# A retention and Fourier-mixing kernel: all work behind the first batch goes onto one written list, the third batch multiplies by seven half-size products in two of three groups, and masks are multiplied in place in f16

## The chip, the cores and the metric

The kernel runs on one core of a Trainium2 chip. The metric is the device time of one execution in microseconds (us). The core has five engines: TensorE (PE in the profile) multiplies matrices, VectorE (DVE) and ScalarE (ACT) work on tiles in SBUF and PSUM, GpSimd (POOL) does elementwise work here and issues a few transfers, and SyncE (SP) issues most of the transfers. Each engine runs its own instructions in order and waits for semaphores of the others.

## The reference

Inputs are q, k and v, each [4 batches, 8 heads, 768 positions, 64], and two weights, w_ch1 [512, 2048] and w_ch2 [2048, 512], all f32. The output is [4, 768, 512] in f32.

```python
gamma = 1 - 2 ** (-5 - arange(8)); scale = 1 / 8
for t in range(768):                       # per batch and head
    state = gamma * state + outer(k[t], v[t])
    y[t] = scale * q[t] @ state
x = heads of y side by side                # [4, 768, 512]
mixed = real(fft(fft(x, axis=1), axis=2))
u = x + mixed
un = (u - mean(u)) / sqrt(var(u) + 1e-6)   # over the 512 columns
out = u + relu(un @ w_ch1) @ w_ch2
```

## The kernel before, in words

The rows of a batch are six blocks of 128. A batch passes through these stages; the letters in brackets are those that the list of the change uses for the same work.

Retention, for each of four pairs of heads. `load_unit` (l) loads q, k and v of the pair by three transfers on the queue of SyncE into buffers of the pool `inp`. `cast_unit` (k) casts them to f16 on GpSimd, k with its decay (L441). `t_unit` (t) transposes q and k to `qT` and `kT`; for the first two batches mostly on TensorE with a copy on ScalarE, for the last two by two transposing transfers issued on SyncE's queue (`qTz<-q16z`, L612, and `kT<-kd`, L614). `kv_unit` (s) makes the running state of each block of rows, `wkK` on TensorE and the sum on VectorE (L696). `a_unit` (a) makes the scores in three parts: two matmuls of 256 columns into `wkA` (L667), and VectorE multiplies the 512 columns in PSUM with a f32 mask into the f16 tile `atm` (L670). `y_unit` (y) multiplies the state and the masked scores with q and v (L717, L721), and ScalarE puts the result into `x` (L729).

The Fourier transform. VectorE folds x by its symmetries (fs, fd, fe; L746, L773, L787, L789 with the tile `ee`), `s1_unit` (f) multiplies along the rows (L850), a small matmul makes the zero column (g), ScalarE or VectorE copies the product and its mirrored copy (gr), and `s2_unit` (x) multiplies along the model dimension into `pq` (L1012), with two copies `qn` on ScalarE (L1014), two operations on VectorE that write `u` (L1019 is the first), and two additions of x on GpSimd (L1040, L1042).

The normalisation. `norm_unit` takes statistics on VectorE (n; L1051, L1052) and ScalarE writes the f16 tile `un` (u; L1056). `unT_unit` (U) transposes `un` to `unT`, by TensorE in the earlier batches, by a transposing transfer on SyncE's queue (L1075) later. `rstd_unit` (r) makes the square root and its reciprocal, which are applied at the end.

The two layers. In the first batch `h0_unit` (i; L1109) and then `h_unit` (h; L1092) multiply `unT` with w_ch1: a unit of h makes 128 hidden columns of 384 rows by four matmuls of 384, and the relu goes to ScalarE (L1096) or VectorE (L1098), by the constant `ACT_ROWS`. Batches of this form have two halves of 384 rows. `ch_unit` (c; L1131) multiplies the hidden tile `ht` with w_ch2: four matmuls of 512 columns for each of four parts of a block of rows; VectorE adds u (L1135), and the block is stored through the pool `obp`. The fourth batch has another form: three groups of 256 rows. `hp_unit` (H; L1179) makes two hidden blocks of 256 rows by eight matmuls of 256, with one relu over both (L1184, split in two for the last block of a group). The 256 rows of a group and the 2,048 hidden columns are then treated as a matrix of 2 by 2 blocks, and so is w_ch2, and the product is made from seven half-size products (`p_unit`, p; L1231, eight matmuls of 256 columns each) in place of eight. This needs sums of hidden blocks (`hidden_sums`, L1203), differences of weight blocks (`wsum_unit`, w; L1165, in spare buffers of `inp`), and sums of the products (add, L1235).

What sets the order. The first batch's retention and Fourier work follow a list, `FIRST`, one unit after the other on every engine. Everything behind it is handed to `emit`: each batch's work is a set of streams, each stream has a start and an end as fractions of a batch (the constants `DM0`, `TS0`, `DA1` and their like), the units of all streams are sorted by these times and handed over in that order, and the framework's scheduler may still reorder instructions where nothing depends on them. The casts of all batches and everything of the fourth batch's own two layers, sums and mixing are `held`: each instruction stays behind the instruction of the same engine that stood before it when it was handed over. While the two layers of one batch run, the retention and Fourier work of the next lies between them. The loads of the third and fourth batch wait for the scores of the second pair of the batch before (`a_of`).

Of the kernel before, what the change touches and what calls it, by code (L numbers as in the profile page):

```python
# [11 lines left out]
AF = mybir.ActivationFunctionType  # L12
# [7 lines left out]
P = 128  # L20
# [27 lines left out]
ON_ACT = {'q': (0, 1, 0), 'kv': (1, 1, 1), 'g': (0, 1, 1), 'gr': (0, 0, 0)}  # L48
# [3 lines left out]
TS1 = (-0.040, -0.020, 0.048, 0.585)  # L52
DA0, DA1 = (0.043, 0.161, 0.176, 0.190, 0.284, 0.321), (0.063, 0.067, 0.063, 0.158, 0.168, 0.189)
LD0, LD1 = (0.223, 0.312), (-0.370, 0.140)
HT0 = (0.666, 0.693, 0.632, 0.590)
NPE = 2
WS = (-0.12, -0.02)
# [3 lines left out]
NT = 0.6  # L61
ACT_ROWS = ((2, 5, 6, 7, 8, 9, 10, 14), (0, 3, 6, 7, 9, 10, 11, 12, 14, 15))
# [3 lines left out]
def kernel(  # L66
# [13 lines left out]
    def pool(name, bufs, **kw):  # L80
# [3 lines left out]
    inp = pool("inp", 11)  # L84
# [12 lines left out]
    obp = pool("obp", 3)  # L97
# [52 lines left out]
    def held(unit):  # L150
        def run():
            ins = tc.nc.cur_bb.bb.instructions
            n0 = len(ins)
            unit()
            for n in range(n0, len(ins)):
                m = n - 1
                while m >= 0 and ins[m].engine != ins[n].engine:
                    m -= 1
                if m >= 0:
                    tc.add_manual_dep(ins[n], ins[m].name,  # L160
                                      mybir.DependencyInfo(mybir.DependencyClass.NoSync,
                                                           mybir.DependencyReason.DATA),
                                      reason="casts in turn")
        return run
# [20 lines left out]
    in_of, a_of = {}, {}  # L185
# [420 lines left out]
    def t_unit(b, i):  # L606
        def run():
# [9 lines left out]
            for dst, src in ((qT, q16_of[b, i]), (kT, kd_of[b, i])):  # L617
# [15 lines left out]
                else:  # L633
                    nc.scalar.copy(dst, tq)
        return run

    def a0_unit(b, i, half):
        def run():
            st = at[b, i]
            hp = PAIR_ORDER[i]  # L640
# [848 lines left out]
```

## Time and profile before

| | |
|---|---|
| median of 3 runs | 241.32 us (241.08 to 241.86) |
| the profiled execution | 240.73 us |
| its span, from the first to the last instruction | 238.7 us |
| instructions | 5575 |
| matmuls on TensorE | 2135 |
| operations on VectorE | 460 |
| operations on ScalarE | 273 |
| operations on GpSimd | 148 |

The page of the profile gives the busy time of each engine, the span in forty slices of about 6 us, the chain of work that ended last, and groups of instructions. A group's row has the line of the code, the engine, the operation, the output and input tiles with their shapes, the count, the busy time in us, the mean duration of one in ns, and the idle time of the engine just before, with what ended it. Views of the trace give the same groups by exact shape, what an engine waited for, a list of a chain's parts with their start and length, and the transfers with the time from issue to landing. In the groups of transfers, the three numbers behind the count are the minimum, median and maximum in ns.

### The profile page before, as it was taken

The numbers are of one execution on the slowest core, as the hardware profiler recorded it, in microseconds if no ns is written. First come the engines' busy times: TensorE is split into PE (matmuls) and PEld (weight loads), VectorE is DVE, ScalarE is ACT, GpSimd is POOL, SyncE is SP. The second block draws the span as 40 slices with busy tenths as digits, with TensorE's granted clock in tenths as the row PEclk, the third lists the DMA queues.
The fourth block names the chain that finished last, engine by engine and source line by source line (L and its number), as shares of the span: only waits on it lengthen the run. The fifth ranks groups of instructions, "written<-read, shape, count | busy, mean of one in ns | idle before, by whom it ended". The sixth has DMA issues, their size and how long they took to land.

```text
span 238.7 us, 5575 instructions
## 1 busy us (share of the span) xinstructions
PE 225.4 (94%) x2135; PEld 155.3 (65%) x2135; DVE 187.4 (79%) x460; ACT 125.3 (52%) x273; POOL 81.4 (34%) x148
## 2 busy tenths in 40 slices
PE   0788999999999999999999999999999999999993
PEld 0356779756775646765567446655666468888893
DVE  8789887958898889986886829977895885867473
ACT  5989759674865444840247415822257326072430
POOL 8378802665300097850000826940002410220000
PEclk9999999999999999999999999999999999999999
DMA  7999999999999489979999577696100261031202
GB/s 179 233 270 239 237 206 207 210 251 248 241 235 208 72 191 221 203 138 132 249 279 218 116 161 203 130 138 156 53 3 0 45 154 25 3 110 23 91 0 91
DMA packets 100954, 36.80 MB, mean 154 GB/s; under 512 B 91456, under 2 KB 97984, under 8 KB 100928
## 3 DMA queue, kind: packets, MB, share of 16 engines
q1 hardware_dynamic: 96704, 32.25, 64.2%
q0 software_dynamic: 4224, 4.19, 10.6%
q8 instruction: 17, 0.28, 0.5%
q14 instruction: 9, 0.07, 0.1%
HBM read 27.26 MB, written 6.29 MB: 141 GB/s over the span
## 4 chain that ended last, share of the span: by engine, by line
PE 82%; DVE 6%; DMA 5%; ACT 2%; issue 1%; POOL 1%; SPq 0%; DVEq 0%; ACTq 0%
PE psc L1131 23%; PE psh L1092 21%; PE psh L1179 9%; PE ps L1231 5%; PE psh L1109 3%; PE wkA L667 3%; DMA qTz<-q16z 3%; PE ps L850 3%; DMA k<-in_k_dram 2%; PE wkY L721 2%; PE pq L1012 2%; PE ps L830 1%; DVE atm L539 1%; PE wkY L717 1%; PE wkK L686 1%
## 5 line engine op out<-in xcount | busy, mean ns | idle before, releaser
L1131 PE MATMUL psc<-w,ht 128*128 128x512 f16 x288 | 67.7, 379 | 0.0
L1092 PE MATMUL psh<-unT,w 128*128 128x384 f16 x320 | 59.5, 326 | 0.0
L1040 POOL TENSOR_TENSOR u<-u,x 128x256 f32<-128x256 f32 x21 | 13.3, 635 | 117.1 <-DVE u L1019 104.8
L1131 PEld LDWEIGHTS <-ht 128*128 128x128 f16 x288 | 27.3, 98 | 26.5
L1092 PEld LDWEIGHTS <-w 128*128 128x128 f16 x320 | 29.9, 98 | 15.9 <-DMA unT<-un 0.4
L1096 ACT ACTIVATE ht<-psh 128x384 f16<-128x384 f32 x46 | 22.3, 489 | 23.7 <-PE psh L1092 23.2
L670 DVE TENSOR_TENSOR atm<-wkA,maskp 128x512 f16<-128x512 f32 x36 | 23.6, 680 | 1.7 <-PE wkA L667 1.7
L1184 ACT ACTIVATE ht<-psh 128x512 f16<-128x512 f32 (+1 forms) x24 | 13.7, 571 | 15.6 <-PE psh L1179 11.0
L1179 PE MATMUL psh<-unT,w 128*128 128x256 f16 x192 | 21.6, 273 | 0.0
L1098 DVE TENSOR_SCALAR ht<-psh 128x384 f16<-128x384 f32 x34 | 18.7, 549 | 2.7 <-PE psh L1092 2.5
L1056 ACT ACTIVATE un<-u,stats 128x512 f16<-128x512 f32 x21 | 14.8, 717 | 10.7 <-DVE stats L1052 7.6
L1179 PEld LDWEIGHTS <-w 128*128 128x128 f16 x192 | 18.7, 98 | 2.1
L1135 DVE SCALAR_TENSOR_TENSOR ob<-psc,stats,u 128x512 f32<-128x512 f32 x18 | 13.4, 743 | 8.5 <-PE psc L1131 8.3
L696 DVE SCALAR_TENSOR_TENSOR s<-s,gk,wkK 128x128 f16<-128x128 f16 x48 | 16.1, 336 | 2.4 <-ACT s L692 1.6
L729 ACT ACTIVATE x<-wkY,gexp 128x384 f16<-128x384 f32 x24 | 12.9, 580 | 9.0 <-PE wkY L721 8.9
L1051 DVE BATCH_NORM_STATS2 bst<-u 128x6 f32<-128x512 f32 x21 | 14.4, 686 | 4.0 <-POOL u L1042 3.8
L1231 PEld LDWEIGHTS <-ht 128*128 128x128 f16 x152 | 14.1, 98 | 2.3 <-issue 0.6
L441 POOL TENSOR_SCALAR kd<-k,gexp 128x384 f16<-128x384 f32 x24 | 13.8, 585 | 3.3 <-DMA k<-in_k_dram 3.3
L667 PE MATMUL wkA<-qTz,kT 128*128 128x256 f16 x72 | 13.2, 273 | 0.3 <-DMA qTz<-q16z 0.3
L1042 POOL TENSOR_TENSOR u<-u,x 128x256 f32<-128x256 f32 x21 | 13.3, 635 | 0.0
L1014 ACT COPY qn<-pq 128x128 f32<-128x128 f32 x18 | 4.9, 274 | 15.0 <-PE pq L1012 15.0
L1203 DVE TENSOR_TENSOR ht<-ht 128x512 f16<-128x512 f16 (+2 forms) x21 | 8.1, 385 | 5.9 <-ACT ht L1184 5.6
(194 smaller groups left out, 400.9 us busy)
## 6 DMA issues: line engine op xcount, KB each, us to landing
q<-in_q_dram SPq DMA_DIRECT2D x16, 384.0 KB, 6.0
k<-in_k_dram SPq DMA_DIRECT2D x16, 384.0 KB, 5.6
v<-in_v_dram SPq DMA_DIRECT2D x16, 384.0 KB, 5.7
out_dram<-ob SPq DMA_DIRECT2D x23, 256.0 KB, 2.4
w<-in_moe_w_ch_dram POOLq DMA_DIRECT2D x8, 512.0 KB, 10.9
unT<-un SPq DMA_TRANSPOSE x15, 2.5
kT<-kd SPq DMA_TRANSPOSE x10, 3.0
qTz<-q16z SPq DMA_TRANSPOSE x8, 3.8
```

The costliest lines, as they stand in the source:

```text
L441: kc = nc.gpsimd.tensor_scalar(out=kd[:, :, h2, :], in0=k32[:, h2], scalar1=gkd[:, h0 + h2:h0 + h2 + 1], scalar2=1.0, op0=ALU.mult, op1=AL ...
L667: mm = nc.tensor.matmul(wk[:, c2], st["kT"][:, c, :], st["qT"][:, :, c, :], start=True, stop=True)
L670: nc.vector.tensor_tensor(out=st["atm"][:, 2 * part:2 * part + 2], in0=wk, in1=maskp[:, PAIR_ORDER[i]].unsqueeze(1).to_broadcast([P, 2, 2, ...
L696: nc.vector.scalar_tensor_tensor(out=s16[:, c], in0=s16[:, c - 1], scalar=gk2[:, hp:hp + 1], in1=wk[:, c - c0], op0=ALU.mult, op1=ALU.add)
L1051: nc.vector.bn_stats(bst, u[:, kb, :])
L1056: nc.scalar.activation(un, u[:, kb, :], AF.Identity, bias=stats[:, kb, 0:1], scale=-1.0)
L1092: nc.tensor.matmul(psh, w116[:, cb, fb * P:(fb + 1) * P], unT[:, cb, rt * 384:(rt + 1) * 384], start=(cb == 0), stop=(cb == 3))
L1096: nc.scalar.activation(ht16[:, fb, :], psh, AF.Relu, bias=0.0, scale=-1.0)
L1098: nc.vector.tensor_scalar(out=ht16[:, fb, :], in0=psh, scalar1=-1.0, scalar2=0.0, op0=ALU.mult, op1=ALU.max)
L1131: nc.tensor.matmul(psc, ht16[:, fb, rb3 * P:(rb3 + 1) * P], w216[:, fb, :], start=(fb == 0), stop=(fb == NFB - 1))
L1179: nc.tensor.matmul(psh[:, t], w116[:, cb, fb * P:(fb + 1) * P], unT[:, cb, g * 256:(g + 1) * 256], start=(cb == 0), stop=(cb == 3))
L1231: nc.tensor.matmul(dst, lhsT, rhs[:, c0:c1], start=bool(new and n == 0), stop=(n == 7), skip_group_check=True)
```

## The change

The streams, `emit` and their constants are gone. In their place stands a second list, `LATER`, of 567 small units, in three parts that are divided by a bar. The units of the first part are pinned on every engine in the written order; those of the second part only on GpSimd; those of the third part are `held`, on every engine and on SyncE's queue. The third part begins where the first batch's last output products and the second batch's hidden units meet. A unit's name is its letter, the batch, and further digits for pair, part, group or block; the letter behind @ names the engine that does its copy, relu or mask (a for ScalarE, v for VectorE, b for one half each, s for ScalarE in two halves, d for a transposing transfer). So a300 is the first third of the scores of pair 0 in batch 3, tq30 the transpose of its q, H207 the last hidden unit of group 0 of batch 2, and p201 product 1 of that group. Batches are counted from 0 in these names.

What the units do changes as follows.

- The second and third batch take the form of `hp_unit`: three groups of 256 rows with matmuls of 256 columns, in place of two halves of 384.
- The third batch (batch 2 in the names) uses the seven products in groups 0 and 1, and full products in group 2 (`cg_unit`, C, with `rows_unit`, O). The second batch uses full products in all groups, and the fourth the seven in all groups, as before. The weight differences are made while the second batch runs.
- In the third and fourth batch the masks are done in two steps. ScalarE copies the scores from PSUM to f16 with the scale of each head (two copies of 256 columns for each part), and one operation on VectorE for a pair (`m_unit`, m) multiplies the 1,536 columns in place with one f16 mask, `mask16`. The second batch's pairs keep the f32 mask on VectorE, now a100@v and its like.
- The transposing transfers of q and k are units of their own (`td_unit`; tq and tk), and loads no longer wait for the scores of the batch before.
- `inp` has 7 buffers in place of 11; four tiles' worth of fixed space, `wide`, takes part of the loads of the first batches and then holds the weight differences. `obp` has 2 buffers in place of 3.
- Which engine does a relu or a copy is written at each unit; the sums of hidden blocks (j) and of products (q) are units of their own.

In the counts of instructions: TensorE has 2311 matmuls after, for 2135. Matmuls of 512 columns at L1131 go from 288 to 224, of 384 from 320 to 64, of 256 for hidden units from 192 to 576, and of the seven products' form from 152 to 264 (some of them narrower in the fourth batch's last group, as before). Masks on VectorE from PSUM go from 36 to 12, beside 8 new products of 1,536 columns, and ScalarE gets 48 scaled copies. Relus on ScalarE: 46 to 10 of 384 columns, 27 to 53 of 512, 3 to 29 of 256. Relus on VectorE: 34 to 6 of 384, 6 to 13 of 512, 3 to 7 of 256. SyncE's and GpSimd's instructions keep their number. TensorE's order of matmuls is the same for the first 710.

```diff
+LATER = """
+i00 i01
+|
+i02 i03 U01@v i10 i11 i12 Z i13 U02@a x03 i20 x04 n03 u03 x05 n04 u04 n05 u05 i21 i22 l10 i23
+l11 r00 c0000 l12 k10 c0001 l13 c0002 U03@a c0003 c0010 t10 U04@v c0011 c0012 MK U05@a k11 c0013
+s100 s101 c0020 t11 a100@v c0021 a101@v c0022 a102@v k12 s110 s111 c0023 y100 y101 t12 a110@v
+h010@a a111@v a112@v h011@v k13 s120 s121 h012@v y110 y111 t13 h013@a a120@v a121@v h014@v
+a122@v s130 s131 h015@v PZ y120 y121 h016@a fs10 h017@a fd10 h018@v a130@v h019@a a131@v h01A@a
+a132@v y130 y131 fs11 fd11 g10 fe10 TB fe11 h01B@a h01C@a h01D@v h01E@a l20 f100@a gr10@v h01F@a
+g112 f110@a gr12@v f101@a c0100 c0101 c0102 f111@a r01 c0103 x10 gr13@v gr11@v x11 n10 u10 x12
...
+u11 u12 k21 U10@v U11@a tq21 tk21 x13 r10 c0123 s200 H101@v H100@v s201 H102@a U12@v a200@a
+a201@a a202@a H103@s m2006 l23 s210 H105@v H104@a y200 s211 y201 a210@a H106@a H107@a k22 n13
+a211@a a212@a m2106 u13 U13@d tk22 C1000 C1001 tq22 C1002 k23 C1003 O100 C1010 y210 C1011 C1012
+x14 s220 y211 tk23 s221 tq23 C1013 n14 a220@a x15 H110@s a222@a H113@b a221@a O101 m2206 H111@v
...
+C1100 C1101 y220 r11 y221 w10 l30 y231 C1102 C1103 w20 fs20 w40 C1110 O110 y230 fs21 g20 C1111
+fd21 C1112 H123@a C1113 O111 fd20 fe20 H120@a w11 w21 H122@a fe21 r12 H124@a w41 f200@a H125@a
+w30 H121@a f201@v w31 gr20@a gr21@v f210@a f211@a H127@a g212 gr22@v x20 H126@a x21 C1200 gr23@v
+C1201 C1202 l31 C1203 n20 u20 U20@d n21 u21 U21@d k30 tk30 tq30 x22 C1210 C1211 C1212 C1213 O120
+k31 tq31 tk31 O121 x23 l32 s300 s301 H201@b H202@a n23 a300@a a301@a a302@a m3006 H200@s s310
+H203@a H204@a k32 n22 u22 s311 H205@a r20 j20106 j20206 j20406 H206@s U22@d a310@a H207@b a311@a
+j20168 a312@a j20268 j20306 y300 y301 tq32 tk32 p201 q201 m3106 q204 u23 x24 j20368 p204 p205
+p206 U23@d q206 l33 p202 q202 j20468 q205 y310 s320 y311 k33 tq33 tk33 a320@a p207 q207 p203
+q203 a321@a n24 u24 H211@v s321 H210@a a322@a m3206 x25 H213@a H214@s H212@a s330 s331 H215@a
+a330@a j21106 a332@a a331@a n25 m3306 U24@d H216@a j21206 H217@s j21306 y321 y320 j21406 j21168
...
+r30 j30406 j30268 p301 u33 U33@d q301 j30368 p304 j30306 p305 j30468 x34 p306 p302 q306 q305
+q302 x35 p307 p303 q303 n34 H312@a H310@a u34 H314@a H311@a H315@s q307 H313@a n35 H316@a j31106
...
+WIDE = 2
 FB = 1
-DM0, DM1 = (0.183, 0.205, 0.286, 0.408), (0.004, 0.137, 0.232, 0.341)
-TS0 = (0.228, 0.358, 0.398, 0.465, 0.512, 0.573, 0.684, 0.694)
-LAST_MIX = {3: (0.0, 0.07, 0.09, 0.20), 4: (0.25, 0.34, 0.36, 0.45), 5: (0.37, 0.445, 0.51, 0.56)}
-SUMS = ((3, 7), (2, 5, 7))
...
-    inp = pool("inp", 11)
+    inp = pool("inp", 7)
...
-    obp = pool("obp", 3)
+    obp = pool("obp", 2)
...
+    mask16 = gk5[:, 1].rearrange("p e c -> p (e c)").bitcast(f16)[:, 0:P]
+    s4t = const.tile([P, 8, P], f16, tag="s4")
...
+    wide = const.tile([P, 4, 2, NCH, D], f32, tag="wide")
+    loads = [0]
+
+    def in_tile(name, b):
+        n = loads[0] % 11
+        loads[0] += 1
+        if b <= WIDE and n >= 7:
+            return wide[:, n - 7]
+        return inp.tile([P, 2, NCH, D], f32, tag="in32", name=f"{name}32")
...
-                if b > 1:
-                    tc.add_manual_dep(dma.ins, a_of[b - 1, 1].ins.name,
-                                      mybir.DependencyInfo(mybir.DependencyClass.Sync,
-                                                           mybir.DependencyReason.DATA),
-                                      reason="loads behind the transposes")
...
+    def td_unit(b, i, part):
+
+        def run():
+            if part == 0:
+                qT = qts[i % 2]
+                nc.sync.dma_start_transpose(qT.rearrange("p h c t -> p (h c) t"),
+                                            q16_of[b, i].rearrange("p h c d -> p (h c d)"))
+            else:
+                kT = tp.tile([P, NCH, P], f16, tag="kT", name="kT")
+                at[b, i] = dict(kT=kT, qT=qts[i % 2])
+                nc.sync.dma_start_transpose(kT, kd_of[b, i].rearrange("p c h d -> p (c h d)"))
+        return run
+
+    def a_unit(b, i, part, eng):
         def run():
             st = at[b, i]
             if part == 0:
@@ -664,75 +681,80 @@
             wk = ps_g.tile([P, 2, 2, P], f32, tag="g", name="wkA")
             for c2 in range(2):
                 c = 2 * part + c2
-                mm = nc.tensor.matmul(wk[:, c2], st["kT"][:, c, :], st["qT"][:, :, c, :],
-                                      start=True, stop=True)
-            a_of[b, i] = mm
+                nc.tensor.matmul(wk[:, c2], st["kT"][:, c, :], st["qT"][:, :, c, :],
+                                 start=True, stop=True)
+            if eng == "v":
+                nc.vector.tensor_tensor(
+                    out=st["atm"][:, 2 * part:2 * part + 2], in0=wk,
+                    in1=maskp[:, PAIR_ORDER[i]].unsqueeze(1).to_broadcast([P, 2, 2, P]),
+                    op=ALU.mult)
+                return
+            for h2 in range(2):
+                nc.scalar.activation(st["atm"][:, 2 * part:2 * part + 2, h2, :], wk[:, :, h2],
+                                     AF.Copy, bias=0.0,
+                                     scale=float(gam[2 * PAIR_ORDER[i] + h2] ** (-P)))
+        return run
+
+    def m_unit(b, i, c0, c1):
+
+        def run():
+            atm = at[b, i]["atm"][:, c0:c1].rearrange("p c h t -> p (c h) t")
             nc.vector.tensor_tensor(
...
+                out=atm, in0=atm,
+                in1=mask16.unsqueeze(1).to_broadcast([P, 2 * (c1 - c0), P]), op=ALU.mult)
...
+    def cg_unit(b, g, t, part):
+
+        def run():
+            rb = 2 * g + t
+            if part == 0:
+                psc_of[b, rb] = ps_pm.tile([P, DM], f32, tag="pm", name="psc")
+            for fb in range(4 * part, 4 * part + 4):
+                nc.tensor.matmul(psc_of[b, rb], hg[:, fb % 8, fb // 8, t * P:(t + 1) * P],
+                                 w216[:, fb, :], start=(fb == 0), stop=(fb == NFB - 1))
...
+            for t0, t1, e in {"a": ((0, 2, "a"),), "v": ((0, 2, "v"),),
+                              "b": ((0, 1, "a"), (1, 2, "v")),
+                              "s": ((0, 1, "a"), (1, 2, "a"))}[eng]:
+                relu(hg[:, n, t0:t1], psh[:, t0:t1], e)
...
+    def sum_unit(b, g, m, n0, n1):
+
+        def run():
+            a11, a12 = hg[:, n0:n1, 0, 0:P], hg[:, n0:n1, 1, 0:P]
+            a21, a22 = hg[:, n0:n1, 0, P:256], hg[:, n0:n1, 1, P:256]
+            s1, s2 = sg[:, 0, n0:n1], sg[:, 1, n0:n1]
+            out_, x, y, op = {1: (s1, a21, a22, ALU.add), 2: (s2, s1, a11, ALU.subtract),
+                              3: (a21, a11, a21, ALU.subtract),
+                              4: (s4t[:, n0:n1], a12, s2, ALU.subtract)}[m]
...
+    for n, part in enumerate(LATER.split("|")):
+        for name in part.split():
+            if n < 2:
+                later_unit(name)()
+                behind()
+                pin((None, ["Pool", "GpSimd"])[n])
+            else:
+                held(later_unit(name))
```

More of the change, by code (lines that the diff above doesn't have):

```diff
@@ new lines, in run @@
+            if half == 0:
+                st["s16"] = sp.tile([P, NCH - 1, P], f16, tag="s16", name="s16")
+            s16 = st["s16"]
+            c0, n = ((0, 3), (3, 2))[half]
+            wk = ps_g.tile([P, 3, P], f32, tag="g", name="wkK", padded_shape=[P, 4, P])
+            for c in range(c0, c0 + n):
+                nc.tensor.matmul(wk[:, c - c0, :], kd[:, c].rearrange("p a b -> p (a b)"),
+                                 v16[:, c].rearrange("p a b -> p (a b)"),
+                                 start=True, stop=True)
@@ L710, in run @@
+            sl = slice(64 * h2, 64 * h2 + 64)
             for c in range(1, NCH):
[L711 to L718 removed]
```

469 lines of the change are left out of this document (158 added, 311 removed).

## The prediction

> **What bounds the kernel now.** I read the page's busy shares first, then its row of forty slices, then what TensorE itself waited for.
>
> ```profile
> span 238.7 us, 5575 instructions
> PE 225.4 (94%) x2135; PEld 155.3 (65%) x2135; DVE 187.4 (79%) x460; ACT 125.3 (52%) x273; POOL 81.4 (34%) x148
> PE   0788999999999999999999999999999999999993
> PEclk9999999999999999999999999999999999999999
> ```
>
> TensorE is busy for 94% of the span, its clock is granted in full throughout, and after the first four slices it never shows less than nine tenths until the last one. So after the first batch the kernel lasts as long as TensorE's list of matmuls plus the holes in it. The holes are few (the columns are total, times, longest):
>
> ```profile
> PE tq L499 <- POOL q16z L456: 5.6, 1, 5.6
> PE ps L1231 <- DVE u L1235: 0.4, 1, 0.4
> PE wkA L667 <- DMA qTz<-q16z: 0.3, 1, 0.3
> PE ps L850 <- DVE ee L787: 0.2, 1, 0.2
> ```
>
> The first is the start of the kernel, which the change leaves as it is. The other three are all that TensorE visibly waits for in 200 us. A change can win here in two ways only: less matmul work, or those 0.9 us.
>
> **The matmul work.** The price of a matmul is read from stretches of the chain in which nothing else interrupts (start, length, what):
>
> ```profile
> 132.08 10.36 PE psc L1131 x48
> 149.34 1.95 PE psh L1092 x12
> 194.40 7.00 PE psh L1179 x64
> ```
>
> That is 0.216 us for 512 columns, 0.1625 us for 384 and 0.109 us for 256. The counts before stand in the groups:
>
> ```profile
> L1131 PE MATMUL psc<-w,ht 128*128 128x512 f16 x288 | 67.7, 379 | 0.0
> L1092 PE MATMUL psh<-unT,w 128*128 128x384 f16 x320 | 59.5, 326 | 0.0
> L1179 PE MATMUL psh<-unT,w 128*128 128x256 f16 x192 | 21.6, 273 | 0.0
> L1231 PE MATMUL ps<-wsum,ht 128*128 128x256 f16 x88 | 11.0, 272 | 0.4 <-DVE u L1235 0.4
> ```
>
> In the changed program I count 224 of the first kind, 64 of the second, 576 of the third, and 112 more 256-wide products of the seven-product form (two more groups of 56). So: -64 x 0.216 = -13.8; -256 x 0.1625 = -41.6; +384 x 0.109 = +41.9; +112 x 0.109 = +12.2. The sum is -1.3 us; with 0.162 for the 384 form it is -1.1. I take **-1.2 us**. Cutting the hidden rows into thirds instead of halves saves nothing, and each of the two groups saves 32 x 0.216 - 56 x 0.109 = 0.8. All other matmuls keep form and number, and up to 65 us into the span TensorE's order is unchanged too.
>
> **The work beside it.** Prices come from these groups:
>
> ```profile
> L670 DVE TENSOR_TENSOR atm<-wkA,maskp 128x512 f16<-128x512 f32 x36 | 23.6, 680 | 1.7 <-PE wkA L667 1.7
> L1098 DVE TENSOR_SCALAR ht<-psh 128x384 f16<-128x384 f32 x34 | 18.7, 549 | 2.7 <-PE psh L1092 2.5
> L1184 ACT ACTIVATE ht<-psh 128x512 f16<-128x512 f32 x21 | 12.5, 597 | 14.8 <-PE psh L1179 10.2 <-issue 4.6
> L1184 ACT ACTIVATE ht<-psh 128x256 f16<-128x256 f32 x3 | 1.1, 383 | 0.8 <-PE psh L1179 0.8
> L1203 DVE TENSOR_TENSOR ht<-ht 128x512 f16<-128x512 f16 x12 | 5.1, 423 | 1.7 <-ACT ht L1184 1.5
> L1165 DVE TENSOR_TENSOR wsum<-w 128x1024 f16<-128x1024 f16 x4 | 2.7, 682 | 0.0
> ```
>
> VectorE loses 24 masks from PSUM (24 x 0.68 = 16.3) and 28 relus of 384 (15.4). It gains eight masks of 1,536 f16 elements, seven relus of 512 (4.7), and the sums and additions of two groups (about 10). No row shows a 1,536-element f16 product. The two f16 rows give 0.26 us for 512 more elements, hence 0.95; at the pace of the f32 row, three times 0.53 plus 0.15, it is 1.74. I take 0.95, since form and type are those of the f16 rows, and keep 1.74 for the range. [...] VectorE in all: -6 us, or about nothing at 1.74.
>
> ScalarE gains 48 scaled copies of 256 (18.4), and its relus cost 8 more: about +27 us, to 152 of 238.7. The tightest stretch is the third batch's first group, from unit a300 to H207's relu: 4 masks in two copies each (3.1), relus (3.7), s310, u22 and the square root (1.3), 8.1 us by durations. Two `un` in a row show that neighbours overlap by 0.1:
>
> ```profile
> 136.63 1.33 ACT L1056 ACTIVATE un<-u,stats 128x512 f16<-128x512 f32 x2 [2.10 <-DVE stats L1052]
> ```
>
> With 18 instructions that leaves 6.3, against TensorE's 6 x 0.875 + 4 x 0.22 + 3 x 0.22 = 6.5 or so. It is hidden, barely: I take 0, and 0.7 as the upper end. GpSimd and the transfers keep their number; only their place changes.
>
> **The two waits that go.** The wait of 0.3 for qTz belongs to a pair of the third batch whose transpose was issued late, behind a load; the written list puts these transposes several units earlier. The wait of 0.4 for u L1235 is in the last batch; the new list puts x34's and x35's work between the products there. I take **-0.7** for both. The 0.2 for `ee` stays, as that stretch is hardly reordered.
>
> **The wait that comes.** Every unit of the list is now fixed in place on every engine, the queue of SyncE included. The queue issues U20, U21, tk30, tq30 in that order, and nothing before a300 can replace them. On TensorE, a300 follows x21 by C1200 to C1213 (32 x 0.216), x22 and x23 (8 x 0.057), s300 and s301 (0.3), H201 and H202 (16 x 0.109): 9.4 us. In that time this must happen:
>
> ```profile
> 133.64 0.45 DVE L1019 SCALAR_TENSOR_TENSOR u<-pq,g,qn 128x256 f32<-128x256 f32 x1
> 134.51 0.64 POOL L1040 TENSOR_TENSOR u<-u,x 128x256 f32<-128x256 f32 x1
> 135.10 0.63 POOL L1042 TENSOR_TENSOR u<-u,x 128x256 f32<-128x256 f32 x1
> 135.77 0.69 DVE L1051 BATCH_NORM_STATS2 bst<-u 128x6 f32<-128x512 f32 x1 [0.49 <-POOL u L1042]
> 133.81 0.72 ACT L1056 ACTIVATE un<-u,stats 128x512 f16<-128x512 f32 x1 [1.09 <-issue]
> ```
>
> ```profile
> L1075 SPq DMA_TRANSPOSE unT<-un x15: 1192/1216/2367, 98.4 to 216.6; - x15
> L614 SPq DMA_TRANSPOSE kT<-kd x8: 1210/1249/1704, 90.5 to 159.0; - x8
> L612 SPq DMA_TRANSPOSE qTz<-q16z x8: 1281/1495/4291, 88.9 to 160.3; - x8
> DMA to landing us min/median/max: 3.7/3.8/7.0
> ```
>
> H126's relu and x21's two copies ahead on ScalarE, 0.8; the first half of u, 0.45; GpSimd, 1.2 and 0.15 behind x20's; statistics 0.7 and their aggregate 0.15; un 0.72; U21 holds the queue 1.22 and tk30 1.25; tq30 lands 3.8 after its issue; some six hand-overs of 0.06, an estimate (from GpSimd's end to the statistics above it is 0.04): 10.8 us. So TensorE stands at a300 for about 1.4 us. All medians of later steps at their minimum give 0.8, and one step less on the chain would give 0. A transpose that is slow to be issued gives more. I take **+1.3**, near the middle of what these rows allow; the ends are 0 and 2.
>
> **The sum.** -1.2 - 0.7 + 1.3 = -0.6 us. The profiled execution took 240.73 us (span 238.7 and 2.0 around it) and becomes 240.1. The median of the runs shown is 241.32, 0.6 above that execution, so **240.7 us** is what I expect of the median: inside or just at what can be told from no change (0.3%, 0.7 us).
>
> **Rivals.** First, faster: the wait at a300 isn't there. For it speaks that other points of the list are timed to a few tenths (tq22 lands, by the same rows, 0.2 to 0.5 us ahead of a220), so the list may fit the chip better than my rows. Then -1.2 - 0.7 remains, and with half of the small holes between 65 and 80 us gone, -2.5: 239.1 us, ranging from 238.3 to 239.8.
>
> Second, slower: the queue of SyncE. The slowest qTz took 4.29 us to be issued and 7.0 to land. It stood right behind a load. In the changed list U22, tq32, tk32 and U23 stand behind l32's three loads, then l33's three loads stand behind U23, and tk33 waits for the cast of l33's keys. From y301, which lets tq32 go, to a330 TensorE has about 13.6 us of work (seven products and six H units of 8 x 0.109 each make 11.3; scores, states and y between them 2.3). The steps are 1.5, 1.25 and 1.22 for three issues, 0.5 for the first load's, 5.6 for the keys' landing, 1.1 for their casts, 1.5 and 1.25 for tq33 and tk33, and 2.9 more until kT has landed, 1.65 of it behind its issue:
>
> ```profile
> k<-in_k_dram SPq DMA_DIRECT2D x16, 384.0 KB, 5.6
> L441 POOL TENSOR_SCALAR kd<-k,gexp 128x384 f16<-128x384 f32 x24 | 13.8, 585 | 3.3 <-DMA k<-in_k_dram 3.3
> ```
>
> Together 15 us at the medians if every step follows the last, and 13.5 if tq33's issue lies under the key casts and the load lands in 5. One issue of 4.29 here costs 2.8 more. The price is 1.5 to 3 us: 242.2 to 243.7, decided where kT of pair 3 lands more than 13.6 us after y301. The list's fixed order speaks for it; that only one of eight qTz was so slow speaks against it.
>
> [...] Two operations of VectorE that read two SBUF tensors took 1.07 us while GpSimd was at work, where 384 elements else take 0.36:
>
> ```profile
> 17.54 1.07 DVE L763 TENSOR_TENSOR xab<-x 128x387 f16<-128x387 f16 x2
> 16.96 1.17 POOL L370 TENSOR_SCALAR ssn<-ssp 128x1158 f16<-128x1158 f16 x1
> L763 DVE TENSOR_TENSOR xab<-x 128x384 f16<-128x384 f16 x6 | 1.9, 356 | 0.2
> ```
>
> The masks before read PSUM and one SBUF tensor; the new ones and the sums of the third batch read two, and lie among GpSimd's casts. If some eleven of them wait 0.3 each and three places have no slack, TensorE loses about 1.2 us more: 241.9. [...]
>
> **Chances.** My forecast 0.42, its own range 239.9 to 241.7, half of it under -0.7; no wait at a300 0.22; the queue 0.26; the port 0.10. Faster by over 0.3%: 0.21 + 0.22 = 0.43. Within: 0.19 and a little of the port's, 0.21. Slower: the rest, 0.36. The range runs from 238.5 to 242.9: it leaves out the best of the first rival and the worst of the second.
>
> **What would show it.** Right: TensorE's waits list wkA with qTz once for over 1 us near 143 to 146 us; no wait of ps for u of 0.4 or more in the last batch; ScalarE near 152 us busy; the mask row near 0.95 us. Wrong: no such wait, or one of over 2 us at a pair of the last batch with loads just ahead on the queue, or ps waiting for u in the third batch; a mask row of 1.7 us would unsettle the count of VectorE.

## The result, and the profile after

The changed kernel took 247.53 us in the median (247.27 to 247.68, 4 runs), the kernel before 241.2 us (4 runs). The ratio is 1.026, with a 95% interval of 1.023 to 1.029: 6.3 us slower. The profiled execution took 247.68 us, with a span of 245.9. Of the runs below, two executions of 335.2 and 335.9 us, with a mean granted clock of 0.66 and 0.67, are left out of the medians.

The page after, its busy shares and the first rows of the forty slices:

```profile
span 245.9 us, 5977 instructions
PE 225.7 (92%) x2311; PEld 172.5 (70%) x2311; DVE 185.9 (76%) x450; ACT 144.8 (59%) x339; POOL 84.2 (34%) x148
PE   0888999999999998997999996979799999999993
PEclk9999999999999999999999999999999999999998
```

No engine is busier than before in a way that would explain 6 us: ScalarE, which gained most, is busy for 59% of the span. The clock is granted in full until the last slice. What is new in TensorE's row are an eight, a six and three sevens among the nines of slices 16 to 29, about 92 to 178 us. What TensorE waited for, asked for four stretches of the changed kernel (65 to 105, 105 to 125, 140 to 155 and 155 to 180 us; total, times, longest):

```profile
PE wkY L742 <- DVE atm L702: 0.7, 1, 0.7
PE ps L871 <- DVE ee L809: 0.2, 1, 0.2
...
PE wkA L684 <- DMA qTz<-q16z: 2.0, 2, 1.7
...
PE wkA L684 <- DMA qTz<-q16z: 2.1, 1, 2.1
...
PE wkK L718 <- POOL v L479: 1.8, 2, 1.6
PE wkA L684 <- DMA kT<-kd: 1.4, 2, 1.3
```

That is 8.2 us, where the kernel before had 0.9 behind its 65th us: 7.3 more. With 1.2 less of matmul work, 6.1 are explained of the 7.2 by which the two profiled spans differ (the medians differ by 6.3); 1.1 stay open. So the kernel didn't become heavier. Apart from the 0.2 for `ee`, which was there before, it became late in six places, and five of them (a220, a230, a300 and the last two pairs), with 7.3 us, wait for transposes of q and k or casts of v.

The chain shows how the largest of these looks (start, length, what):

```profile
138.32 0.23 PE pq L1025 x4
138.55 3.45 PE psc L1158 x16
142.00 0.23 PE pq L1025 x4
142.24 3.45 PE psc L1158 x16
...
146.21 3.80 DMA qTz<-q16z
150.15 0.81 PE wkA L684 x6
```

and SyncE's queue over the same time and a little later, when the last two pairs are fetched:

```profile
142.29 2.50 SPq L1088 DMA_TRANSPOSE unT<-un  x2
144.89 1.23 SPq L673 DMA_TRANSPOSE kT<-kd  x1
146.21 1.46 SPq L668 DMA_TRANSPOSE qTz<-q16z  x1
...
154.33 1.65 SPq L237 DMA_DIRECT2D v<-in_v_dram  x1
156.08 3.45 SPq L1088 DMA_TRANSPOSE unT<-un  x1
159.64 1.46 SPq L668 DMA_TRANSPOSE qTz<-q16z  x1
162.04 1.21 SPq L673 DMA_TRANSPOSE kT<-kd  x1
163.34 1.22 SPq L1088 DMA_TRANSPOSE unT<-un  x1
```

tq30, which a300 needs, is issued behind U20, U21 and tk30, and lands 3.8 us later. U22 stands right behind the three loads l32 and holds the queue for 3.45 us in place of 1.2, with tq32 and tk32 of the fourth batch's third pair behind it, and behind these U23 and the loads l33 of the last pair. The third pair waits for the kT of tk32, which then had to wait for its casts too, since l32 itself came late in the queue:

```profile
160.16 1.85 POOL L474 TENSOR_SCALAR kd<-k,gexp 128x384 f16<-128x384 f32 x2 [1.51 <-DMA k<-in_k_dram]
```

GpSimd stood 1.5 us for the keys of l32; its two casts end at 162.01 and tk32 goes at 162.04. The loads of the last pair go behind that, at 164.62.

### The profile page after: what moved, and what is told of

Read it like the earlier page. It is cut to its first block, busy times and chain, and to the rows that moved or that the text cites. A ratio compares the mean times of both kernels' runs of the same rounds, so it can differ in the third digit from the quotient of the medians.

```text
span 245.9 us, 5977 instructions
## 1 busy us (share of the span) xinstructions
PE 225.7 (92%) x2311; PEld 172.5 (70%) x2311; DVE 185.9 (76%) x450; ACT 144.8 (59%) x339; POOL 84.2 (34%) x148
## 4 chain that ended last, share of the span: by engine, by line
PE 74%; DMA 9%; DVE 5%; issue 3%; POOL 3%; ACT 3%; SPq 2%; DVEq 0%
PE psh L1200 21%; PE ps L1249 11%; PE psc L1158 10%; PE psc L1145 7%; DMA qTz<-q16z 5%; PE psh L1110 4%; PE psh L1123 3%; DMA v<-in_v_dram 3%; PE wkA L684 3%; PE ps L871 3%; PE wkY L742 2%; PE ps L852 1%; PE pq L1025 1%; PE wkY L739 1%; DMA kT<-kd 1%
## 5 line engine op out<-in xcount | busy, mean ns | idle before, releaser
L1200 PE MATMUL psh<-unT,w 128*128 128x256 f16 x576 | 68.0, 273 | 0.0
L1103 ACT ACTIVATE ht<-psh 128x512 f16<-128x512 f32 (+2 forms) x92 | 46.5, 523 | 36.4 <-PE psh L1200 28.0
L1200 PEld LDWEIGHTS <-w 128*128 128x128 f16 x576 | 55.7, 98 | 6.8
L1158 PE MATMUL psc<-w,ht 128*128 128x512 f16 x128 | 29.3, 379 | 0.0
L1249 PEld LDWEIGHTS <-ht 128*128 128x128 f16 x248 | 23.2, 98 | 2.6
L1145 PE MATMUL psc<-w,ht 128*128 128x512 f16 x96 | 22.8, 379 | 0.0
L1158 PEld LDWEIGHTS <-ht 128*128 128x128 f16 x128 | 12.1, 98 | 12.8
L1218 DVE TENSOR_TENSOR ht<-ht 128x768 f16<-128x768 f16 (+1 forms) x30 | 12.3, 425 | 8.7 <-ACT ht L1103 8.3
L693 ACT ACTIVATE atm<-wkA 128x256 f16<-128x256 f32 x48 | 15.0, 397 | 6.7 <-PE wkA L684 6.7
L1100 DVE TENSOR_SCALAR ht<-psh 128x512 f16<-128x512 f32 (+2 forms) x26 | 15.0, 580 | 3.4 <-PE psh L1200 1.5
L1249 PE MATMUL ps<-wide,ht 128*128 128x256 f16 x120 | 15.5, 272 | 0.0
L1145 PEld LDWEIGHTS <-ht 128*128 128x128 f16 x96 | 9.1, 98 | 8.5
L702 DVE TENSOR_TENSOR atm<-atm,gk 128x1536 f16<-128x1536 f16 x8 | 8.8, 1100 | 7.4 <-ACT atm L693 7.4
```

The costliest lines, as they stand in the source:

```text
L693: nc.scalar.activation(st["atm"][:, 2 * part:2 * part + 2, h2, :], wk[:, :, h2], AF.Copy, bias=0.0, scale=float(gam[2 * PAIR_ORDER[i] + h2 ...
L1100: nc.vector.tensor_scalar(out=dst, in0=src, scalar1=-1.0, scalar2=0.0, op0=ALU.mult, op1=ALU.max)
L1103: nc.scalar.activation(dst, src, AF.Relu, bias=0.0, scale=-1.0)
L1145: nc.tensor.matmul(psc_of[b, rb], ht16[:, fb, rb3 * P:(rb3 + 1) * P], w216[:, fb, :], start=(fb == 0), stop=(fb == NFB - 1))
L1158: nc.tensor.matmul(psc_of[b, rb], hg[:, fb % 8, fb // 8, t * P:(t + 1) * P], w216[:, fb, :], start=(fb == 0), stop=(fb == NFB - 1))
L1200: nc.tensor.matmul(psh[:, t], w116[:, cb, fb * P:(fb + 1) * P], unT[:, cb, g * 256:(g + 1) * 256], start=(cb == 0), stop=(cb == 3))
```

## The experiments

Three theories were set against each other. Q: the order of SyncE's queue and of the casts that feed it makes the loss. M: the masks in place do. S: the seven products of the third batch do. All runs stand beside runs of the kernel before on the same chip, and the ratios are to those. Only the list is edited unless the text says otherwise; the diffs show the stretches of it that matter, without its line breaks.

**One pair earlier.** k30, tk30 and tq30 are moved in front of x20.

```diff
-n21 u21 U21@d k30 tk30 tq30 x22
+g212 gr22@v k30 tk30 tq30 x20
```

> Three units of the list are moved: the casts and the two transposes of the fourth batch's first pair (k30 tk30 tq30) stand ahead of x20, where GpSimd idles for 25 us and SyncE's queue for 8, in place of behind U20 and U21; nothing else. Theory Q (what the changed kernel loses, it loses because the transposes of q and k stand in SyncE's queue behind transposes of un that aren't ready and behind loads): TensorE's wait of 2.2 us at a300 goes, and everything that follows on the queue comes 2.8 us earlier while TensorE comes 2.2 earlier, so the waits behind it (1.8 at pair 2, 2.1 at pair 3) keep 0.6 less each at most: 244.5 us, from 243.3 to 245.3. Theory M (the masks in place, with their copies on ScalarE and their operation on VectorE, hold the chain from scores to y) and theory S (the seven products of the third batch, with their sums on VectorE, hold it): the time is not set by this wait and it returns elsewhere, 247.0 to 247.7.

245.81 us, ratio 1.018 (1.015 to 1.022), above the range of theory Q. The wait at a300 is gone, but only 1.7 of the forecast 3 us came back: a wait of 1.1 us for `ee` appeared, which ends at 133.4 us. VectorE's fold `eo`, first in the changed kernel and then here (minimum, median and maximum in ns), and GpSimd's casts here:

```profile
L795 DVE TENSOR_TENSOR eo<-xab x4: 551/552/556, 128.5 to 130.9; 128x768 f16<-128x768 f16 x4
```

```profile
L795 DVE TENSOR_TENSOR eo<-xab x12: 545/552/1174, 71.8 to 185.9; 128x768 f16<-128x768 f16 x12
```

```profile
128.43 1.36 POOL L471 TENSOR_SCALAR q16z<-q 128x384 f16<-128x384 f32 x2 [15.06 <-issue]
131.19 1.12 POOL L479 TENSOR_SCALAR v<-v 128x768 f16<-128x768 f32 x1
```

The casts now lie among the folds. Three of the four folds there took 0.84 to 1.17 us in place of 0.55, and the cast of v 1.12 in place of 0.83. GpSimd was idle there, and yet the place was not free.

**The third batch's transposes ahead of un.**

```diff
-n13 a211@a a212@a m2106 u13 U13@d tk22 C1000 C1001 tq22 C1002 k23 C1003
+n13 a211@a a212@a m2106 u13 tk22 tq22 k23 U13@d tk23 C1000 C1001 C1002 C1003
...
-x14 s220 y211 tk23 s221 tq23 C1013
+x14 s220 y211 tq23 s221 C1013
```

> Units of the third batch's retention are moved in the list: tk22, tq22 and the casts k23 stand ahead of U13, tk23 directly behind U13, tq23 directly behind y211. Theory Q: the waits of 0.5 us at a220 and 1.9 at a230 go, and since the later waits hang on work that follows TensorE, they stay as they are: 245.2 us, from 244.7 to 246.3. Theories M and S: 247.0 to 247.7.

245.88 us, ratio 1.019 (1.015 to 1.022). The wait for qTz between 100 and 125 us fell from 2.0 to 0.5 us, and the others stayed within 0.1 us, as theory Q has it. Most of it had been at a230, for tq23: this transpose landed 5.5 us after its issue, where the median is 3.8. In this run it took 5.3, but was issued 1.4 us earlier. Why it lands so late is not shown.

**The masks back to f32.**

```diff
-a200@a a201@a a202@a H103@s m2006
+a200@v a201@v a202@v H103@s
```

> The masks of the third and fourth batch go back to one operation on VectorE for each part, from PSUM with the f32 mask; the copies on ScalarE and the eight units m are gone. VectorE gets 24 x 0.68 and loses 8 x 1.1 (7.5 us more), ScalarE loses 48 copies (15 us). Theory M: the time falls by 2 us or more, below 245.5. Theory Q: only the wait of 0.8 at the first pair's y (a mask that took 2.1 us in place of 0.95 beside GpSimd's casts) goes, and the queue's waits stay: 246.7, from 246.2 to 247.7. Theory S: 246.5 to 249, by what VectorE's added work does.

246.26 us, ratio 1.020 (1.016 to 1.023), 1.3 below the changed kernel. The waits for qTz at a300, for kT and for v are still 2.1, 1.7 and 1.4. Theory M as the main cause falls. But the masks were not free: the wait at y200 is gone, and the 2.0 us at a220 and a230 are down to 0.7. In the changed kernel four copies for the masks, 1.2 us, stand on ScalarE right in front of u13; without them U13 and all that stands behind it on the queue went 1.0 us earlier (102.31 in place of 103.33).

**Full products in the third batch.** The p, q and j units of groups 0 and 1 become eight C and two O each.

```diff
-tq32 tk32 p201 q201 m3106 q204 u23 x24 j20368 p204 p205 p206 U23@d q206 l33 p202
+tq32 tk32 C2000 m3106 u23 x24 C2001 C2002 C2003 O200 U23@d l33 C2010
```

> The third batch's groups 0 and 1 get full products (eight parts C and two O for each group) in place of the seven with their sums and additions; the list is otherwise the same. TensorE's work grows by 2 x 0.8 us, VectorE's falls by about 10. Theory Q: group 0's 0.8 is swallowed by the waits at pair 2 and 3 of the fourth batch, which the queue sets, group 1's is not: 248.3, from 247.6 to 249.1. Theory S: VectorE's sums were in the way, and the time falls: below 246.5. Theory M: 249.1, both groups' work in full.

251.69 us, ratio 1.042 (1.038 to 1.047): 4.2 above the changed kernel, more than any theory had. Theory S falls. What goes beyond the matmul work came in the profiled run from the clock (0.66 and 0.68 in two stretches of 5 us), told of in the last section.

**Two transposes of un taken out of the queue.** U22 and U23 become U22@a and U23@a, done by TensorE.

> U22 and U23, two transposes of un that stand in SyncE's queue between the last batch's loads and its transposes of q and k, are done by TensorE with a copy on ScalarE; all else is as in the changed kernel. TensorE's work grows by about 0.5 us. Theory Q: the queue loses 3.5 us of issue ahead of tq32 and 1.2 ahead of the loads l33, so the waits at the fourth batch's pairs 2 and 3 (3.9 us together) fall to below 1.5: 245.5 us, from 244.7 to 246.6. Rival L: these waits hang on the loads' landing and their place in the list, not on the queue in front of them, and stay: 247.5 to 248.5.

246.25 us, ratio 1.020 (1.016 to 1.024). Between 155 and 180 us only this is left of the 3.2 us of waits:

```profile
PE wkK L718 <- POOL v L479: 0.2, 1, 0.2
```

All four runs lie below what the rival L forecast, so the queue in front of the last pairs has a part in these waits. How large it is, this run doesn't show: the median fell by 1.3 us and not by 3.0, and in the profiled run a lower clock from 150 to 155 us (0.66) made TensorE 1.7 us later, which by itself gave the queue more time.

**The f16 masks alone, in the kernel before.**

```diff
             a_of[b, i] = mm
+            if b >= NPE:
+                for h2 in range(2):
+                    nc.scalar.activation(st["atm"][:, 2 * part:2 * part + 2, h2, :], wk[:, :, h2],
+                                         AF.Copy, bias=0.0,
+                                         scale=float(gam[2 * PAIR_ORDER[i] + h2] ** (-P)))
+                if part == 2:
+                    atm = st["atm"].rearrange("p c h t -> p (c h) t")
+                    nc.vector.tensor_tensor(
+                        out=atm, in0=atm,
+                        in1=mask16.unsqueeze(1).to_broadcast([P, 2 * NCH, P]), op=ALU.mult)
+                return
```

> The kernel before, with one part of the change alone: the masks of the third and fourth batch in two steps, copies on ScalarE and one f16 operation on VectorE for a pair; streams, order, 384-column hidden units and full products as before. Theory Q: the masks alone cost little, 241.5 us, from 240.6 to 242.6. Theory M: they cost 2 us or more of the 6.3: above 243.

245.94 us, ratio 1.020 (1.016 to 1.024). In the old order the masks alone cost 5 us. What TensorE waited for behind 65 us:

```profile
PE wkY L733 <- DVE atm L678: 1.2, 2, 0.9
PE psh L1104 <- DVE ht L1110: 0.7, 2, 0.3
PE psh L1104 <- ACT ht L1108: 0.6, 1, 0.6
```

In the kernel before, the part of y that needs the masks starts 0.8 to 3.0 us behind the last scores of its pair, in the changed kernel 3.2 to 10: in the old order the copies and the mask of a pair stand more in its way, and three relus are late too. These rows are 2.5 us of the 3.9 by which this profiled execution exceeds that of before; the rest stays open, and so does whether the shorter distance is the cause, as no run changed it alone. So M is a small part in the changed list (1.3 us) and a large one in the old order: the price of the same operations depends on the order that they stand in.

**All queue fixes at once.** All loads early, casts behind them, each transpose of q and k ahead of those of un, and y211, H106 and H112 moved a few places.

```diff
-y211 tk23 s221 tq23 C1013
+y210 y211 tq23 l30 C1011 C1012 x14 s220 s221 C1013
...
-w10 l30 y231
+U14@d l31 n15 k30 k31 ... U15@d tk30 tk31 ... y221 tq30 w10 y231 tq31 l32 l33
...
-U21@d k30 tk30 tq30 x22
+U21@d x22
...
-y300 y301 tq32 tk32
+a302@a tk32 ... a312@a tk33 ... y300 y301 tq32
```

> Order alone is changed, in the third part of the list: all loads of the fourth batch (l30 to l33) are issued before 130 us, while the queue is idle; the casts k30 and k31 follow them, k32 and k33 come before they are needed; each transpose of q and k stands ahead of the transposes of un, at the first place where its buffer is free; y211 and two hidden units of the third batch are moved by a few places to cover the first two pairs. No operation is added or taken away. Theory Q: TensorE's waits of 8.5 us in sum go: 239.5 us, from 238.5 to 241.0, so at or below the kernel before. [...]

251.26 us, ratio 1.040 (1.036 to 1.044). Here tq31 was put ahead of y230, which still reads that buffer, so that part of the third batch is computed with the wrong q, and TensorE waited 9.3 us for it. The same slip is in the next run, the same list with l32 and l33 where the changed kernel has them: 252.03 us, ratio 1.044 (1.040 to 1.048). With that wait in them, neither time says anything on the theories.

> As e7_all, but l32 and l33 with their casts and transposes stay where the changed kernel has them (behind x23 and behind q206). Theory Q with the loads as the larger part: the waits at the fourth batch's pairs 2 and 3 stay at 2 to 4 us, and the kernel is that much slower than e7_all: 242.5, from 241.5 to 244. If the transposes in front of them were the larger part, it is within 1 us of e7_all.

Both were repeated with tq31 behind y230:

> As e7_all with one unit moved back: in e7_all the transpose tq31 stood ahead of y230, the last reader of the buffer that it fills, so that y230 took the wrong q and waited 9.3 us for it; here tq31 and the loads behind it follow y230. Theory Q as for e7_all: TensorE's 8.5 us of waits go and no other comes: 239.7 us, from 238.5 to 241.2. Theory G (casts beside VectorE's folds): 1 to 3 us of them come back as waits for ee or the masks: 241.2 to 243.

243.42 us, ratio 1.009 (1.006 to 1.013). It is above the ranges of both theories. None of the six waits is left, and theory G's waits for `ee` or the masks didn't come, but between 100 and 160 us there are two new ones, of 1.3 us for U15 and of 2.3 for U20 and U21, and for the first SyncE's queue shows why:

```profile
PE psh L1200 <- DMA unT<-un: 3.6, 2, 2.3
```

```profile
118.94 1.91 SPq L237 DMA_DIRECT2D v<-in_v_dram  x1
120.95 3.38 SPq L1088 DMA_TRANSPOSE unT<-un  x1
```

Now U15 stands right behind a load and holds 3.38 us, as U22 did before. U20 goes at 143.27, behind the loads l32 and l33 and a store; in the next run, where these loads stand later, it goes at 141.32.

> As e7b_all, but l32 and l33 with the casts and transposes of their pairs stay where the changed kernel has them. If the late loads are a cause by themselves, TensorE waits for the last pair's casts of v and for its transposes, 1.5 to 4 us: e7b_all plus 2, from plus 1 to plus 4. If the other transposes in the queue were all of it, within 0.7 us of e7b_all.

242.06 us, ratio 1.005 (1.003 to 1.007). The expected loss against e7b_all did not come. The last pair waits 1.1 us for v, but the queue is free for U20 and U21, and 1.7, at U15, is left of the 3.6. Early loads are no gain by themselves; what counts is that none stands in front of a transpose that is due.

> As e7b_all, with the masks of the third and fourth batch as f32 masks on VectorE from PSUM. Theory Q: with the queue out of the way TensorE's work sets the time in both, and the masks' form makes less than 1 us: 239.7, from 238.9 to 241. Theory M (the kernel before with the f16 masks alone took 5 us longer than before): the f16 masks cost 2 us or more in this order too, and the time falls below e7b_all by that.

243.78 us, ratio 1.015 (1.010 to 1.020), too near to e7b_all to tell the two apart. The f32 masks were not faster, so theory M falls here too; theory Q's 239.7 didn't come either.

**The loads spread.**

```diff
-tq23 l30 C1011 ... U14@d l31 n15 k30 k31 ... U15@d tk30 tk31 ... y221 tq30 w10
+tq23 l30 C1011 ... U14@d n15 k30 ... U15@d tk30 ... y221 tq30 l31 w10
-O110 y230 tq31 l32 l33 fs21
+O110 l32 y230 fs21
-U21@d x22 C1210 C1211 C1212 C1213 O120 O121 x23 s300
+U21@d tk31 tq31 x22 k32 C1210 C1211 C1212 C1213 O120 O121 l33 x23 s300
```

> Order alone is changed again, from the same operations: as e7b_all, but the loads are spread so that none stands directly in front of a transpose of un. l30 is issued behind tq23, l31 behind tq30 (so behind U15), l32 behind the store of O110, l33 behind the stores of O120 and O121 (so behind U20 and U21); the casts k31, k32, k33 and their transposes follow at the next place after. Theory Q: the two waits for unT that took over in e7b_all (1.4 and 2.5 us) were the queue's again, 3.4 us of issue behind a load for U15 and loads ahead of U20; they go, and TensorE keeps less than 1 us of waits behind 65 us: 239.1 us, from 238.3 to 240.6, faster than the kernel before by 0.2 to 1%. Rival R: the retention work of the fourth batch doesn't fit into this time in any order, because the queue or GpSimd has too little room; a wait of 1 us or more comes at another pair or block: 240.6 to 242.5.

241.12 us, ratio 1.002 (1.000 to 1.005), level with the kernel before. That is the rival's range and not theory Q's. One wait of TensorE above half a us is left behind 65 us:

```profile
PE wkA L684 <- DMA qTz<-q16z: 1.6, 1, 1.6
```

**And its last wait covered.** a320 is moved behind p203 and q203.

> As e11_spread, with a320 moved from in front of p207 to in front of a321, two products later, so that 1.7 us of TensorE's work lie in the wait for tq32. If the matmul term holds (1.2 us less work than before, and nothing else in the way): the wait goes, 239.4 us, from 238.8 to 240.2, faster than the kernel before by 0.3 to 0.9%. If a wait takes its place at a321, a322 or s330: 240.5 to 241.2, no difference from the kernel before.

239.95 us, ratio 0.996 (0.995 to 0.998): faster than the kernel before. The same kernel again, for its profile:

> The kernel of e12_a320_later once more, for its profile: span near 238.0 us, and behind 65 us no wait of TensorE above 0.5 us; its last matmul ends near 233.5, 1.4 us ahead of the kernel before (234.9).

239.8 us, ratio 0.992 (0.989 to 0.995). The page's first rows, and then what TensorE waited for behind 65 us:

```profile
span 238.1 us, 5978 instructions
PE 224.7 (94%) x2311; PEld 172.6 (72%) x2311; DVE 186.5 (78%) x450; ACT 143.8 (60%) x339; POOL 83.5 (35%) x148
```

```profile
PE ps L1249 <- DVE u L1263: 0.5, 2, 0.3
PE psh L1200 <- DVE ht L1100: 0.2, 1, 0.2
PE ps L871 <- DVE ee L809: 0.2, 1, 0.2
```

With the operations of the changed kernel and only their order changed, the waits are back at 0.9 us, as in the kernel before, and the time is about 7.6 us below the changed kernel. The gain against the kernel before, 1.0 and 1.3 us in the two sets, is about the matmul term of the prediction; between the two profiled executions it is smaller, 0.6 us of span and 0.7 of TensorE's busy time, and the last matmul ends at 234.4, 0.5 us ahead and not 1.4. A transpose right behind a load is still there: tk32 holds the queue for 3.88 us at 150.29. TensorE waits for nothing behind it, because nothing behind it is due so soon.

**What the parts are worth where nothing waits.** e12_a320_later with full products, and with f32 masks:

> As e12_a320_later, with full products in both groups of the third batch in place of the seven. By the matmul term alone TensorE's work grows by 2 x 0.8: 241.0 us, 1.6 above e12_a320_later, from 1.2 to 2.2. If the sums and additions on VectorE ate the saving, the two are within 0.5 us. A wait of TensorE of over 2.2 us, after which the clock was halved for 3.3 us in e5_no_seven, should not be there.

242.23 us, ratio 1.005 (1.003 to 1.007): 2.3 us above e12_a320_later, a little over the range. TensorE waits for 0.4 us behind 65 us, so the seven products are worth at least their matmul work, 1.6; the other 0.7 stay open.

> As e12_a320_later, with f32 masks on VectorE for the third and fourth batch. By the prediction's terms VectorE has 7.5 us more and ScalarE 15 less, and both lie beside TensorE: within 0.7 us of e12_a320_later. By theory M the f16 masks cost time in any order: faster than it by 1 us or more. By e4_f32_masks and e10_all_f32_masks, where VectorE came late with relus and u: slower by 0.5 to 1.5.

243.02 us, ratio 1.008 (1.005 to 1.011): 3.1 us above it, more than any of the three ranges. Without the f16 masks VectorE is late:

```profile
PE ps L1249 <- DVE u L1263: 1.3, 1, 1.3
PE psh L1200 <- DVE ht L1100: 1.1, 1, 1.1
PE ps L1249 <- DVE ht L1100: 0.6, 1, 0.6
PE ps L1249 <- DVE ht L1218: 0.4, 2, 0.2
```

In this order the f16 masks gain 3 us, where they cost 5 in the old one and 1.3 in the changed kernel.

## Why the prediction was wrong

**The matmul work was right.** The counts came as counted, and at the prices used the sum is the same -1.2 (with 0.162 for the 384 form too, where the prediction wrote -1.1). In e12_a320_later and e12_look, the same kernel, the time is lower by 1.0 and 1.3 us; e12_look's waits are as in the kernel before. e13_no_seven shows the saving of the seven products. The groups of the hidden layer, after the change:

```profile
L1200 PE MATMUL psh<-unT,w 128*128 128x256 f16 x576 | 68.0, 273 | 0.0
L1110 PE MATMUL psh<-unT,w 128*128 128x384 f16 x64 | 12.6, 326 | 0.3 <-ACT ht L1103 0.3
```

**The work beside it was right in price for the masks, and once late.** The eight masks were forecast at 0.95 us:

```profile
L702 DVE TENSOR_TENSOR atm<-atm,gk x8: 948/958/2110, 96.0 to 177.5; 128x1536 f16<-128x1536 f16 x8
```

and GpSimd beside the slow one:

```profile
96.53 0.83 POOL L479 TENSOR_SCALAR v<-wide 128x768 f16<-128x768 f32 x1
```

The median is 0.958; one took 2.11. It starts at 96.0, GpSimd's casts run until 97.36, and y200 waits 0.7. The third rival counted on such slow operations, with three tight places and 1.2 us in all; on VectorE it was one place. (Its pair of slow operations took 1.07 us together, 0.35 more than twice the usual 0.36.) It left out the other side: GpSimd's two casts of keys at 160.16 took 1.85 us, where one takes 0.585 at the median, while a mask ran from 160.05 for 0.95, and tk32 waited for them. ScalarE was forecast near 152 us and had 144.8. VectorE was forecast 6 us lower and fell by 1.5, to 185.9; the terms as written add up to about -9, not -6. The sum of the prediction used neither.

**The two waits that go: one did.** The 0.4 for u is no longer among the waits. The 0.3 for qTz was at a pair of the third batch, and among that batch's pairs it grew to the 2.0 at a220 and a230.

**The wait that comes: right mechanism, too small.** 1.3 us were forecast at a300, and 2.1 measured. From the end of x21's matmuls (138.55 in the chain) to tq30's landing (146.21 and 3.80 later) it took 11.5 us, where the prediction counted 10.8.

**The sum is the step that failed.** It took one new wait at one pair, +1.3, where the changed kernel waits 7.3 us more than the kernel before, and left the others to rivals, as if only one of them could come true. The queue rival was priced at 1.5 to 3 us and given 0.26; it came with 3.2 at the last two pairs (kT of pair 3 landed about 17 us after y301, where the rival set the limit at 13.6; its steps as written add up to 15.6, not 15), together with the wait at a300 and the 0.7 at y200. And the 2.0 us at a220 and a230 had no term at all: the first rival used the short lead there (0.2 to 0.5 us) as a sign that the list fits the chip. It was the sign of the opposite, a place without slack. U13 stands in the queue ahead of tk22, tq22, tk23 and tq23 and waits until un is there; with tq23 landing in 5.5 us and not the 3.8 of the prediction's rows, a230 waited 1.7. e3_batch2_queue took 1.5 of the 2.0 us away by putting tk22 and tq22 ahead of U13. Here a written order that holds the queue too turned a transpose that waits for its data into a wait of all behind it. That belonged in the sum as one term for each pair, not as a chance.

## What to carry to other kernels

When a scheduler's freedom is replaced by a fixed order, go through each queue of transfers, not only the engines: for every transfer, ask what stands ahead of it, when that one's data are ready, and how long it holds. Waits of this kind at different places add up, so they belong into the sum, not among the rivals. An idle queue or engine is only a free place if nothing that stands behind it is due, and if the work put there doesn't slow the neighbour's down, as casts did with a mask (2.11 us beside them, 0.95 else).

## What the runs showed of the hardware

**Behind some waits the granted clock of TensorE fell.** In the run with full products two waits of 2.1 and 2.7 us were followed by stretches at a lower clock, 0.66 and 0.68; behind the changed kernel's wait of 2.1 us at a300 the clock stayed at 1.00. The fourth number is the granted clock (start and end, length, busy and matmuls, clock, share of the DMA engines, GB/s):

```profile
145.00:150.00 5.00, 2.98 (x28) 1.00 0.86 184
150.00:155.00 5.00, 4.95 (x32) 0.66 0.99 206
155.00:160.00 5.00, 5.00 (x61) 1.00 1.49 229
...
175.00:180.00 5.00, 4.65 (x33) 0.68 0.48 123
```

0.66 over 5 us is 1.7 us of full clock lost, and 0.68 is 1.6, an estimate from these two rows. Together with 1.6 of work this is 4.9, against the 4.3 by which this execution was slower than the profiled one of the changed kernel. The run without two transposes of un shows the same 0.66 from 150 to 155 us, behind a wait of 2.0. How long the clock was low within these 5 us is not in the rows; at half the clock, the 0.50 that the changed kernel's trace shows from 244.30 us to its end, it would be 3.4, 3.2 and 3.4 us, an estimate from these numbers. So a wait of about 2 us was followed by a lower clock in two runs and not in the changed kernel, nor did one of 2.3 us lower it in e7b_all, whose mean clock was 1.000. What decides it is not shown, and no run was made to test it.

**Operations of VectorE and casts of GpSimd took longer beside each other.** A mask took 2.11 us beside casts and 0.95 else, a fold up to 1.17 beside them and 0.55 else, as shown. On GpSimd two casts of keys took 1.85 in place of 1.2 beside a mask, and a cast of v 1.12 in place of 0.83 beside the folds. What makes them longer is not shown.

**Transposing transfers right behind a load held their queue longer.** Behind the 60th us three transposes were issued within 0.15 us of the end of a load's issue in the traces of the kernel before and of the changed one. They held the queue for 2.37 us (before, at 98.38), 4.29 (before, at 109.12) and 3.45 (after, at 156.08). The one of e7b_all at 120.95, shown above, held it for 3.38. The other transposes of the two traces behind the 60th us took 1.19 to 1.70 us, but for four of 2.02 to 2.47. What makes the difference is not shown.
